# One granule's second FFN product as seven half-size products, in a fused attention and FFN kernel

## The chip, the cores and the metric

The kernel runs on one core of one Trainium2 chip. The metric is the device time in microseconds of one execution. All sets of timed runs here are of the fast state (the one not slowed by a lower TensorE clock), with a granted clock of 0.996 or more; the state of two single looks counts as unknown. The span in a profile is some 1.8 us shorter than the time of the same run. In the text PE is TensorE, PEld its loading of weights, DVE VectorE, ACT ScalarE, POOL GpSimd and SP the engine that issues most transfers, SPq its DMA queue.

## The reference

Attention with global and local keys, then an FFN with a squared relu, on 4 x 768 = 3072 tokens of width 512 and a hidden width of 2048:

```python
scores = q @ k.T / sqrt(64) + bias          # 8 heads; keys: 8 global ones, and the last 96
x = softmax(where(keep, scores, -1e9)) @ v  # heads side by side: 3072 x 512
h = x @ w_in                                # 512 -> 2048
g = s * maximum(h, 0)**2 + b
out = g @ w_out                             # 2048 -> 512
```

## The kernel before

Tokens are worked on in 12 granules of 256 (two blocks of 128). A granule passes through scores (L444), attention product (L504), normalisation on VectorE, a transposition of its result into `xT`, the first FFN product in eight chunks (L632), relu and square, and the second FFN product. From granule 4 on, pairs of granules do the second product in Strassen form (seven products where a plain one has eight, L832), for which sums of quarters of `w_out` (`weight_sums`) and of the data (`g_sum`) are made. Granules 0 to 3 do it plainly (L680). From granule 4 on the transposition is done by DMA:

```python
def x_by_dma(j):
    t = xT_tile(j)
    for i in range(GB):
        nc.sync.dma_start_transpose(t[:, :, i * P : (i + 1) * P], xn[j][:, i, :])

def p2_mm(j, tb, lo=0, hi=FC):              # plain second product of a block: L680
    ...
    for fc in range(lo, hi):
        nc.tensor.matmul(po[:], lhsT=g_of(j)[:, fc, tb * P : (tb + 1) * P],
                         rhs=w_out_bf[:, fc, :], start=(fc == 0), stop=(fc == FC - 1))

def finish_granule(j):
    ...                                     # x_by_pe for j < 4, else x_by_dma
    if 6 <= j + LEAD < NJ:
        hold_loads(xT[j][0:1, 0, GT - 1 : GT])   # GpSimd waits until xT has landed (L122)
        load_granule(j + LEAD)
```

`hold_loads` is of use to the reader: the start of GpSimd's small gate copy shows in the trace when granule j's transposes have landed. A `step(s, c0, c1, c2)` issues: scores of two units for step s+1, `c0`, an attention product, the output work put off until then (`flush`), `c1`, another attention product, `flush`, `c2`; at a granule's last step `finish_granule` comes after the first piece of `c2`. The steps in question:

```python
step(8, [lambda: rest(2, 0)] + late_p1(3, (0,)), late_p1(3, (1, 2)), late_p1(3, (3,)))
step(9, p2[2][1:2], late_p1(3, (4, 5)), late_p1(3, (6, 7)))            # finishes granule 4
step(10, p2[3][0:1], [lambda: shifted_template(range(H))], late[0:2] + [bias_diff], ps_h)
step(11, [lambda: p2_mm(3, 1, 0, FC // 2), u1(4, 0)], [u1(4, 1)],      # u1(4, 0): first use of xT 4
     late[2:4] + [shifted_copy, weight_sums[0]])
step(12, [lambda: rest(3, 1), u1(4, 2)], [weight_sums[1], u1(4, 3)], [weight_sums[2]])
```

The softmax here doesn't subtract the row's maximum and nothing guards it: scores larger than these inputs give would overflow.

## Time and profile before

| | before |
|---|---|
| time, median of 6 runs | 208.6 us (208.38 to 208.85) |
| span of the profile | 206.6 us |
| PE busy | 201.9 us |
| granule 4's first FFN matmul starts | 83.20 us |
| GpSimd's gate copy: granule 4's xT has landed | 82.96 us |

### The profile page before, as it was taken

The numbers are of one execution on the slowest core, as the hardware profiler recorded it, in microseconds if no ns is written. First come the engines' busy times: TensorE is split into PE (matmuls) and PEld (weight loads), VectorE is DVE, ScalarE is ACT, GpSimd is POOL, SyncE is SP. The second block draws the span as 40 slices with busy tenths as digits, with TensorE's granted clock in tenths as the row PEclk, the third lists the DMA queues.
The fourth block names the chain that finished last, engine by engine and source line by source line (L and its number), as shares of the span: only waits on it lengthen the run. The fifth ranks groups of instructions, "written<-read, shape, count | busy, mean of one in ns | idle before, by whom it ended". The sixth has DMA issues, their size and how long they took to land.

```text
span 206.6 us, 5313 instructions
## 1 busy us (share of the span) xinstructions
PE 201.9 (98%) x2182; PEld 160.1 (77%) x2190; DVE 160.9 (78%) x338; ACT 127.8 (62%) x197; POOL 69.9 (34%) x90
## 2 busy tenths in 40 slices
PE   8999999999999999999999999999999999999993
PEld 2678884557867585878888898888888889888883
DVE  7977589977989866799799975699866696737974
ACT  5766669486976558685664595663695764476200
POOL 8986333899454500913700907300000000000000
PEclk9999999999999999999999999999999999999999
DMA  5999999999999999999999999999570300240006
GB/s 163 173 179 201 207 206 178 156 153 130 130 147 119 156 121 218 208 195 214 148 205 149 116 125 212 167 219 77 53 206 3 98 9 0 61 145 0 0 10 197
DMA packets 110836, 28.17 MB, mean 136 GB/s; under 512 B 97852, under 2 KB 109308, under 8 KB 110812
## 3 DMA queue, kind: packets, MB, share of 16 engines
q0 software_dynamic: 76000, 13.11, 85.9%
q1 hardware_dynamic: 33612, 14.13, 41.0%
q10 hardware_dynamic: 1200, 0.59, 1.1%
q8 instruction: 17, 0.28, 0.6%
q14 instruction: 7, 0.06, 0.1%
HBM read 27.26 MB, written 6.29 MB: 162 GB/s over the span
## 4 chain that ended last, share of the span: by engine, by line
PE 95%; DMA 2%; DVE 1%; issue 0%; ACT 0%
PE ps L632 41%; PE ps L832 24%; PE ps L680 13%; PE ps_s L444 6%; PE ps_av L504 5%; DMA first<-in_k_dram 2%; PE ps_s L530 1%; PE ps_t L354 1%; PE ps_x L604 1%; PE ps_t L331 1%; PE ps_s L545 1%; PE ps_s L419 1%; PE ps_av L571 1%; PE ps_last L832 0%; PE ps_t L344 0%
## 5 line engine op out<-in xcount | busy, mean ns | idle before, releaser
L632 PE MATMUL ps<-xT,w_in_bf 128*128 128x256 bf16 x768 | 90.4, 273 | 0.1
L642 ACT ACTIVATE gT<-ps 128x512 bf16<-128x512 f32 x96 | 55.9, 598 | 47.9 <-PE ps L632 47.6
L632 PEld LDWEIGHTS <-w_in_bf 128*128 128x128 bf16 x768 | 73.1, 98 | 9.6 <-DVE xT L607 0.2
L453 ACT ACTIVATE pt<-ps_s 128x1024 bf16<-128x1024 f32 (+1 forms) x44 | 39.3, 946 | 3.2 <-PE ps_s L444 3.0
L680 PE MATMUL ps<-w_out_bf,gT 128*128 128x512 bf16 x120 | 28.7, 380 | 0.5 <-issue 0.2
L460 DVE TENSOR_TENSOR pt<-pt,tmpl 128x1024 bf16<-128x1024 bf16 (+1 forms) x40 | 24.4, 643 | 3.8 <-ACT pt L453 3.7
L832 PEld LDWEIGHTS <-gsum 128*128 128x128 bf16 x256 | 24.2, 98 | 3.7 <-DVE gsum L795 0.5
L108 POOL DMA_DIRECT2D vb<-in_v_dram x24 | 21.5, 910 | 5.5 <-DMA w_out_bf<-in_moe_w_out_dram 3.3
L806 DVE TENSOR_TENSOR gT<-gT 128x1024 bf16<-128x1024 bf16 x20 | 13.7, 686 | 11.7 <-ACT gT L642 11.7
L680 PEld LDWEIGHTS <-gT 128*128 128x128 bf16 x128 | 11.7, 98 | 13.0
L469 DVE TENSOR_TENSOR xn<-ps_av,rc 128x256 bf16<-128x256 f32 x48 | 20.4, 424 | 1.7
L832 PEld LDWEIGHTS <-gT 128*128 128x128 bf16 x200 | 18.6, 98 | 2.3
L468 DVE RECIPROCAL rc<-ps_av 128x4 f32<-128x4 f32 x48 | 8.5, 178 | 12.3 <-PE ps_av L504 10.8
L504 PEld LDWEIGHTS <-pt 128*128 128x128 bf16 x320 | 14.4, 97 | 2.7 <-DVE xn L469 0.7
L645 DVE TENSOR_TENSOR gT<-gT 128x512 bf16<-128x512 bf16 x32 | 13.0, 420 | 3.6 <-ACT gT L642 3.3
L504 PE MATMUL ps_av<-vb,pt 128*128 128x65 bf16 x208 | 15.3, 193 | 0.0
L832 PE MATMUL ps<-w_out_bf,gsum 128*128 128x256 bf16 x128 | 15.3, 273 | 0.0
L832 PE MATMUL ps<-wsub,gsum 128*128 128x256 bf16 x128 | 15.1, 273 | 0.0
L116 POOL DMA_DIRECT2D nat<-in_q_dram x14 | 12.4, 888 | 7.0 <-DMA vb<-in_v_dram 2.7
L122 POOL COPY gate<-xT 1x1 bf16<-1x1 bf16 x6 | 1.5, 250 | 37.1 <-DMA xT<-xn 37.1
L116 POOL DMA_DIRECT2D nat<-in_k_dram x14 | 12.4, 884 | 4.9 <-DMA w_in_bf<-in_moe_w_in_dram 2.4
L832 PE MATMUL ps<-w_out_bf,gT 128*128 128x256 bf16 x120 | 13.9, 273 | 0.0
(111 smaller groups left out, 230.5 us busy)
## 6 DMA issues: line engine op xcount, KB each, us to landing
out_dram<-o_q SPq DMA_DIRECT2D x15, 256.0 KB, 2.6
vb<-in_v_dram POOLq DMA_DIRECT2D x24, 128.0 KB, 8.8
nat<-in_k_dram POOLq DMA_DIRECT2D x22, 128.0 KB, 6.7
nat<-in_q_dram POOLq DMA_DIRECT2D x22, 128.0 KB, 6.9
w_out_bf<-in_moe_w_out_dram POOLq DMA_DIRECT2D x4, 512.0 KB, 16.2
w_in_bf<-in_moe_w_in_dram POOLq DMA_DIRECT2D x4, 256.0 KB, 7.5
w_in_bf<-in_moe_w_in_dram POOLq DMA_DIRECT2D x2, 512.0 KB, 11.2
out_dram<-o_sb SPq DMA_DIRECT2D x4, 256.0 KB, 6.1
```

The lines of the kernel that those rows point to most:

```text
L108: nc.gpsimd.dma_start(vbuf[b % 2][:, sb, :, 0:D], rows_of(v, b, sb))
L116: nc.gpsimd.dma_start(t[:, n, i, :, :], rows_of(srcs[n], b, sb))
L453: nc.scalar.activation(pt[:, :, 0:ncol], ps[:, :, 0:ncol], ACT.Exp, scale=QSCALE)
L460: nc.vector.tensor_tensor(pv, pv, m.rearrange("p h a c -> p h (a c)"), ALU.mult)
L469: nc.vector.tensor_tensor(dst, av[:, :, :, 0:D], rc[:].to_broadcast((P, 2, 2, D)), ALU.mult)
L504: nc.tensor.matmul(av[:, i, hi, 0 : D + 1], lhsT=pt[:, hi, c * P : (c + 1) * P], rhs=vv, start=(n == 0), stop=(n == len(terms) - 1),)
L632: nc.tensor.matmul(ps[:, i, :], lhsT=w_in_bf[:, kc, fc * P : (fc + 1) * P], rhs=xT[j][:, kc, :], start=(kc == 0), stop=(kc == KC - 1),)
L642: nc.scalar.activation(gs, ps[:], ACT.Relu)
L645: nc.vector.tensor_tensor(gs, gs, gs, ALU.mult)
L680: nc.tensor.matmul(po[:], lhsT=g_of(j)[:, fc, tb * P : (tb + 1) * P], rhs=w_out_bf[:, fc, :], start=(fc == 0), stop=(fc == FC - 1),)
L806: outs.append(lambda: nc.vector.tensor_tensor(gs, gs, gs, ALU.mult))
L832: nc.tensor.matmul(ps[:, tb, cs], lhsT=stat[:, fc, tb * P : (tb + 1) * P], rhs=mov[:, fc, cs], start=(fc == 0), stop=(fc == NH - 1),)
```

## The change

Granule 3's two blocks are taken as the two rows of a Strassen product by themselves: 7 products of 8 matmuls with 256 columns replace 2 x 16 matmuls with 512. The weight sums are therefore needed earlier, and so VectorE makes all four in stretches where it was idle. Two squares go to ScalarE, and four late outputs are put off to make room.

```diff
+    def sg_prod(n):
+        ...
+            for fc in range(NH):                       # 8 matmuls with 256 columns: L968
+                nc.tensor.matmul(ps, lhsT=stat[:, fc, :], rhs=mov[:, fc, :], ...)
+            outs.append(lambda: sg_evac(n, ps))
     ...
     finish_granule(2)
+    weight_sums[0]()
     ...
-    step(9, p2[2][1:2], late_p1(3, (4, 5)), late_p1(3, (6, 7)))
-    step(10, p2[3][0:1], [lambda: shifted_template(range(H))], late[0:2] + [bias_diff], ps_h)
+    step(9, [weight_sums[1]] + p2[2][1:2], [sg_sum(3)] + act_p1(3, (4, 5)),
+         late_p1(3, (6,)) + [weight_sums[2]] + late_p1(3, (7,)) + [flush, sg_sum(1)])
+    step(10, [sg_prod(7), sg_prod(1), sg_prod(2)],
+         [bias_diff, lambda: shifted_template(range(H)), sg_prod(5)], [sg_sum(4)], pre=[sg_sum(2)])
     step(
         11,
-        [lambda: p2_mm(3, 1, 0, FC // 2), u1(4, 0)],
-        [u1(4, 1)],
-        late[2:4] + [shifted_copy, weight_sums[0]],
+        [sg_prod(6), u1(4, 0)],
+        [sg_join(1), weight_sums[3], u1(4, 1)],
+        [sg_join(0), sg_join(2), shifted_copy] + late[0:2],
     )
-    step(12, [lambda: rest(3, 1), u1(4, 2)], [weight_sums[1], u1(4, 3)], [weight_sums[2]])
+    step(12, [sg_prod(3), sg_prod(4), u1(4, 2)], [u1(4, 3)], late[2:4])
```

More of the change, by code (lines that the diff above doesn't have):

```diff
@@ L921, in join, with sg_half, sg_sum, go @@
         return go
+    SG = 3
+    sg = {}
+    def sg_half(half, tb):
+        return g_of(SG)[:, half * NH : (half + 1) * NH, tb * P : (tb + 1) * P]
+    def sg_sum(n):
+        def go():
+            if not sg:
+                for i, key in ((2, (3, 1)), (3, (2, 4))):
+                    t = gpool.tile([P, 2, NH, P], BF16, name="sgsum", tag=f"gsum{i}", bufs=1)
+                    for a, m in enumerate(key):
+                        sg[m] = t[:, a]
+            dst, x, y, op = {
+                1: (sg[1], sg_half(0, 1), sg_half(1, 1), ALU.add),
+                2: (sg[2], sg[1], sg_half(0, 0), ALU.subtract),
+                3: (sg[3], sg_half(0, 0), sg_half(0, 1), ALU.subtract),
+                4: (sg[4], sg_half(1, 0), sg[2], ALU.subtract),
+            }[n]
+            nc.vector.tensor_tensor(dst, x, y, op)
+        return go
@@ new lines, with go @@
+    sg_ps = {}
+    sg_r = {}
+    def sg_prod(n):
+        def go():
+            stat = {
+                1: lambda: sg_half(0, 0),
+                2: lambda: sg_half(1, 0),
+                3: lambda: sg[4],
+                4: lambda: sg_half(1, 1),
+                5: lambda: sg[1],
+                6: lambda: sg[2],
+                7: lambda: sg[3],
+            }[n]()
+            mov = {1: w11, 2: w21, 3: w22, 4: t4, 5: t1, 6: t2, 7: t3}[n]
+            bank, c = {1: (0, 0), 7: (0, 1), 2: (1, 0), 5: (2, 0), 6: (4, 0), 3: (3, 0), 4: (3, 1)}[n]
+            if bank not in sg_ps:
+                sg_ps[bank] = ps_h.tile([P, GB, CH], F32, name="ps_2", tag="psh")
+            ps = sg_ps[bank][:, c, :]
+            for fc in range(NH):
+                nc.tensor.matmul(
+                    ps, lhsT=stat[:, fc, :], rhs=mov[:, fc, :], start=(fc == 0), stop=(fc == NH - 1)
+                )
+            outs.append(lambda: sg_evac(n, ps))
+        return go
@@ new lines, in sg_store, with sg_evac @@
+    def sg_store(tb):
+        b, g = divmod(SG, NGR)
+        t0 = b * S + g * GT + tb * P
+        nc.sync.dma_start(out[t0 : t0 + P, :], sg_r["out", tb][:])
+    def sg_evac(n, ps):
+        if not sg_r:
+            p0, p1_, p2_ = (
+                work.tile([P, GB, CH], F32, name=f"part{i}", tag=f"part{i}", bufs=1)
+                for i in range(3)
+            )
+            sg_r.update({0: p0[:, 0, :], 6: p0[:, 1, :], 1: p1_[:, 0, :], 7: p2_[:, 0, :]})
+            for tb in range(GB):
+                sg_r["out", tb] = work.tile([P, DM], F32, name="o_sb", tag="o_sb", bufs=3)
+        if n == 1:
+            scaled(sg_r[0], ps, bvec[:, 0:CH])
+        elif n == 2:
+            scaled(sg_r["out", 0][:, 0:CH], ps, sg_r[0])
+        elif n == 5:
+            scaled(sg_r[1], ps, bdiff[:])
+        elif n == 6:
+            scaled(sg_r[6], ps, sg_r[0])
+        elif n == 7:
+            nc.scalar.activation(sg_r[7], ps, ACT.Copy, scale=s_bc[:])
+        elif n == 3:
+            scaled(sg_r["out", 0][:, CH:DM], ps, sg_r[1])
+            sg_store(0)
+        elif n == 4:
+            scaled(sg_r["out", 1][:, 0:CH], ps, sg_r[6])
+            sg_store(1)
@@ L923, in pe, with sg_join, go @@
+    def sg_join(n):
+        def go():
+            if n == 1:
+                add_f32(sg_r[1], sg_r[1], sg_r[6])
+            elif n == 0:
+                add_f32(sg_r[6], sg_r[6], sg_r[7])
+            else:
+                add_f32(sg_r["out", 1][:, CH:DM], sg_r[7], sg_r[1])
+        return go
     def pe(pr, n):
@@ L942, in go, with act_p1 @@
             outs.append(square)
+        return [lambda fp=fp: go(fp) for fp in fps]
+    def act_p1(j, fps):
+        def go(fp):
+            relu, _ = p1_mm(j, fp)
+            relu()
+            gs = g_of(j)[:, 2 * fp : 2 * fp + 2, :]
+            nc.scalar.activation(gs, gs, ACT.Square)
         return [lambda fp=fp: go(fp) for fp in fps]
@@ L1167 @@
     step(8, [lambda: rest(2, 0)] + late_p1(3, (0,)), late_p1(3, (1, 2)), late_p1(3, (3,)))
-    step(9, p2[2][1:2], late_p1(3, (4, 5)), late_p1(3, (6, 7)))
-    step(10, p2[3][0:1], [lambda: shifted_template(range(H))], late[0:2] + [bias_diff], ps_h)
+    step(
+        9,
+        [weight_sums[1]] + p2[2][1:2],
+        [sg_sum(3)] + act_p1(3, (4, 5)),
+        late_p1(3, (6,)) + [weight_sums[2]] + late_p1(3, (7,)) + [flush, sg_sum(1)],
+    )
+    step(
+        10,
+        [sg_prod(7), sg_prod(1), sg_prod(2)],
+        [bias_diff, lambda: shifted_template(range(H)), sg_prod(5)],
+        [sg_sum(4)],
+        pre=[sg_sum(2)],
+    )
     step(
         11,
-        [lambda: p2_mm(3, 1, 0, FC // 2), u1(4, 0)],
-        [u1(4, 1)],
-        late[2:4] + [shifted_copy, weight_sums[0]],
+        [sg_prod(6), u1(4, 0)],
+        [sg_join(1), weight_sums[3], u1(4, 1)],
+        [sg_join(0), sg_join(2), shifted_copy] + late[0:2],
     )
-    step(12, [lambda: rest(3, 1), u1(4, 2)], [weight_sums[1], u1(4, 3)], [weight_sums[2]])
+    step(12, [sg_prod(3), sg_prod(4), u1(4, 2)], [u1(4, 3)], late[2:4])
     for pr in range(2, NJ // 2):
@@ L1192 @@
             [u1(o, 3), g_sum(pr, 1, 0)],
-            [g_sum(pr, 1, 1), pe(pr, 7), g_sum(pr, 2)] + [weight_sums[3]] * (pr == 2),
+            [g_sum(pr, 1, 1), pe(pr, 7), g_sum(pr, 2)],
             pre=[g_sum(pr, 3, 1)],
```

## The prediction

> **What bounds the kernel now.** I read the page's engine table first, then the chain that ended last, then the same chain in order of time around the second FFN product of granule 3, and last the timelines of VectorE, the transposing DMA queue and GpSimd for the same microseconds.
>
> ```profile
> PE 201.9 (98%) x2182; PEld 160.1 (77%) x2190; DVE 160.9 (78%) x338; ACT 127.8 (62%) x197; POOL 69.9 (34%) x90
> PE 95%; DMA 2%; DVE 1%; issue 0%; ACT 0%
> ```
>
> TensorE (PE) is busy 98% and is 95% of the chain. After the first 5 us nothing holds it up: the list of waits has no PE matmul wait above 0.2 us. So a microsecond of PE work taken away is a microsecond gained, unless PE then arrives too early for something else. The chain in order of time shows the work that the change touches (start, length, what):
>
> ```profile
> 76.49 0.55 PE ps_s L444 x16
> 77.04 0.32 PE ps L680
> 77.36 0.05 issue
> 77.42 3.19 PE ps L680 x14
> 80.60 0.48 PE ps_av L504 x16
> 81.09 0.44 PE ps_s L444 x12
> 81.53 1.62 PE ps L680 x7
> 83.15 0.05 issue
> 83.20 1.91 PE ps L632 x16
> 85.11 0.24 PE ps_av L504 x8
> 85.35 1.75 PE ps L632 x16
> ...
> 87.78 0.16 issue
> 87.94 1.67 PE ps L680 x7
> ```
>
> The L680 pieces are granule 3's product: block 0 from 77.04 to 80.60, the first half of block 1 from 81.53 to 83.20, its second half from 87.78 to 89.61. At 83.20 the first FFN matmul of granule 4 (L632) starts, on an xT that the DMA queue transposes. Two lines say when that xT is there:
>
> ```profile
> 75.45 2.52 SPq L612 DMA_TRANSPOSE xT<-xn  x2
> 82.96 0.47 POOL L122 COPY gate<-xT 1x1 bf16<-1x1 bf16 x1 [12.65 <-DMA xT<-xn]
> ```
>
> The two transposes are issued from 75.45 on, and GpSimd, which sat 12.65 us waiting for the second of them, gets on at 82.96. PE wants it at 83.20, so it is there only 0.24 us before it is needed. That margin is hidden in the profile of before (PE shows no wait), and I take it for the number that decides this case.
>
> **What the Trainium skill says.** "TensorE: Matmul & The Clock Gate", section "Back-to-back issue gap", lists 262 cycles for 256 columns and 518 for 512 at 2.4 GHz, so 109 and 216 ns: halving the columns costs almost nothing. The trace agrees: 16 matmuls of 256 columns take 1.75 us, 109 ns each; block 0's 16 of 512 take 3.56 us, 222 ns. (The same section's sustained figure of 131 ns for 512 columns is not what this trace shows.) "VectorE: DVE Perf Modes", section "The perf-mode tier table", has a bf16 tensor_tensor of 2048 elements at 1224 ns; the weight sums of this trace took 1215 to 1218 ns. "DMA: Bandwidth & Descriptors", section "Issuing engines are not separate DMA queues", says transfers from all issuing engines run on the same 16 DMA engines; the DMA row is at 9 in nearly every slice until two thirds of the span, and the transposes of granule 4 took about 6 us from issue to landing in that crowd.
>
> **The change, part by part.**
>
> *PE, the gain.* Gone are 2 x 16 matmuls of 512 columns: 3.56 + 1.67 + 1.83 = 7.06 us on the chain. Added are 7 products of 8 matmuls of 256 columns: 56 x 109 ns = 6.12 us. The weights loaded rise from 32 to 56, at 98 ns each, under the 109 ns of the matmul beside them. PE work falls by 0.94 us by the chain; by pure pitch it is 8 x 109 = 0.87 us. I use 0.87.
>
> *Where it is gained.* In place of block 0 (3.56 us) PE now does products 7, 1, 2 and 5, 32 x 109 ns = 3.50 us: next to nothing. In place of block 1's first half (1.67 to 1.75 us) it does product 6 alone, 0.87 us: here is the gain. In place of the second half it does products 3 and 4, 1.75 for 1.83 us. So nearly all of the gain falls due just before granule 4's first matmul, which PE would now reach at about 82.35.
>
> *The new wait.* Nothing in the change makes granule 4's transposes earlier. They need the last attention output of granule 4, which VectorE writes from 75.00 (reciprocal at 74.78, both set by PE); what stands before them in that DMA queue is the same. So the xT lands at about 82.9 again, and PE can start at about 83.0 to 83.1 rather than 82.35: some 0.7 us of the 0.87 are lost. Left: 83.20 - 83.05 = 0.15 us, and about 0.07 us from the second half, together 0.2 us.
>
> *VectorE, added.* Between 71.7 and 80 us it gets two weight sums (1.14 us each from start to start, as in the trace), three 1024-element sums (0.60 to 0.68 each) and loses two squares that go to ScalarE (0.75). Idle there was:
>
> ```profile
> 72.79 0.18 DVE L468 RECIPROCAL rc<-ps_av 128x4 f32<-128x4 f32 x1 [1.05 <-PE ps_av L504]
> 74.78 0.18 DVE L468 RECIPROCAL rc<-ps_av 128x4 f32<-128x4 f32 x1 [0.69 <-PE ps_av L504]
> 76.28 0.43 DVE L645 TENSOR_TENSOR gT<-gT 128x512 bf16<-128x512 bf16 x1 [0.19 <-ACT gT L642]
> 77.16 0.42 DVE L645 TENSOR_TENSOR gT<-gT 128x512 bf16<-128x512 bf16 x1 [0.45 <-ACT gT L642]
> 80.88 0.18 DVE L468 RECIPROCAL rc<-ps_av 128x4 f32<-128x4 f32 x1 [1.20 <-PE ps_av L504]
> ```
>
> Following its new order by hand: masks end at 71.67; first sum to 72.81, where the reciprocal was due at 72.79; normalisation and output to 74.03; sum 3 to 74.63, due 74.78; normalisation to 75.34; sum of w12 in place to 76.48; the two last squares, held by their relu, to 77.58; sums 1 and 2 to 79.0; masks to 80.2; normalisation to 80.8. Against PE: product 7 needs the w12 sum at 77.04 (0.5 us to spare), product 2 the squares at 78.8 (1.2), product 5 sum 1 at 79.9 (1.6), and the next attention product needs that normalisation at 80.8 (nothing to spare: a wait of up to 0.1 us, which the xT wait swallows). The evacuations that product 6 and granule 4 wait for come at about 81.1 and 81.4, with 0.4 us or more to spare. The first weight sum, now after granule 2's transposition, takes 1.14 us of a VectorE pause of 1.04 us that ends at 51.26; PE uses that result only from 53.1. The fourth goes from 110 to about 86 us and is due at product 4, near 88.4 (0.8 to spare). To make room, the four late outputs (0.66 us each) are moved back.
>
> *ScalarE.* Two squares, about 0.6 us each, before the relu of the last two chunks; it had pauses of 0.28, 0.52 and 0.28 us, then 77.02 is reached as before. No effect on PE.
>
> *DMA.* The four stores of late outputs now all go behind granule 5's transposes in the queue, where three went ahead. Those transposes landed by 96.24 for a need at 97.64, and now come earlier.
>
> **The rivals.** *(A) The full gain:* the transposes land early enough, because the crowd on the DMA engines happens to clear sooner. Then 208.57 - 0.87 = 207.7. For it: the time to landing is a matter of what else is in flight, and 0.5 us is small beside 6. Against: all traffic ahead of it is unchanged. *(B) VectorE becomes the bound* in the stretch from 76 to 81 us: each step there lies within 0.1 to 0.5 us of its need, and a slip of 0.5 us at product 7 or the attention product adds that much, then 208.6 to 209.0. For it: 78% busy before, and 95% in this stretch after. Against: the hand-made order has PE need each result later than it comes, and the first 0.6 us of such a slip only takes the place of the xT wait. *(C) A slip of the attention output of granule 4* (VectorE held up by the first two sums at 72 to 75 us) moves the transposes and with them granule 4: as much loss as slip, up to 0.3 us, so 208.6 at most.
>
> **Range and chances.** The expected sum is 208.57 - 0.2 = 208.35. Weights by judgement: the xT wait as worked out 0.65, (A) or part of it 0.15, (B) or (C) 0.2. That gives 207.7 to 208.75 for 8 in 10. A gain of 2% would be 4.2 us, over four times the PE work removed: ruled out. A loss of 2% needs a wait of 4 us or more, which nothing in the profile offers.
>
> **What would show it.** In the profile after: PE busy falls by about 0.9 us while the span falls by much less; the 120 recorded matmuls of 512 columns at L680 become some 90, and 56 of 256 appear; PE's list of waits gains one of 0.5 to 0.7 us at L632, put down to the DMA of xT, and GpSimd's gate copy stands again near 83.0 with L632 right behind it. Wrong would be: L632 of granule 4 at 82.4 with no wait (A); a PE wait on VectorE at the new products or at the attention product after them (B); the SP transposes issued later than 75.5 (C).

## More of the kernel before

How full VectorE is in the stretch that the change fills shows in the view of stretches (the columns are the length, then the busy time of PE, PEld, DVE, ACT and POOL; the last three are the granted clock, the DMA engines' share and GB/s):

```profile
70.00:81.00 11.00, 10.95 (x107) 7.12 (x106) 6.63 (x15) 6.67 (x15) 0.31 (x1) 1.00 1.78 171
```

PE is busy for 10.95 of the 11 us, VectorE (third pair) for 6.63.

## The result, and the profile after

The median is 208.5 us (six runs, 207.65 to 209.18) against 208.6 (208.38 to 208.85). The ratio is 0.9994, with a 95% interval of 0.997 to 1.0017. A ratio is the mean time of one kernel's fast runs over that of the other's of the same rounds, so not quite the ratio of the medians. It is the same time within the noise, inside the predicted range. One thing stands out that the prediction had not named: the changed kernel's runs spread over 1.5 us, those of before over 0.5.

The page of the changed kernel:

```profile
PE 201.0 (97%) x2209; PEld 162.0 (78%) x2214; DVE 165.2 (80%) x347; ACT 129.3 (63%) x200; POOL 69.9 (34%) x90
...
PE 92%; DMA 5%; DVE 1%; issue 0%; SPq 0%
...
L632 PE MATMUL ps<-xT,w_in_bf 128*128 128x256 bf16 x768 | 90.4, 273 | 0.7 <-DMA xT<-xn 0.7
```

PE is busy 0.9 us less, and the span is no shorter (206.8 us). The DMA's share of the chain rose from 2% to 5%, and the first FFN product has an idle time of 0.7 us ahead of it, ended by the DMA of xT, where it had 0.1:

```profile
L632 PE MATMUL ps<-xT,w_in_bf 128*128 128x256 bf16 x768 | 90.4, 273 | 0.1
```

PE's timeline shows where (start, length, what; in brackets the idle time before and what ended it), and GpSimd's and the queue's say why:

```profile
77.05 1.05 PE L968 MATMUL ps<-w_out_bf,sgsum 128*128 128x256 bf16 x8
77.94 1.91 PE L968 MATMUL ps<-w_out_bf,gT 128*128 128x256 bf16 x16
...
79.93 1.03 PE L968 MATMUL ps<-wsub,sgsum 128*128 128x256 bf16 x8
...
81.71 1.05 PE L968 MATMUL ps<-wsub,sgsum 128*128 128x256 bf16 x8
83.42 1.91 PE L632 MATMUL ps<-xT,w_in_bf 128*128 128x256 bf16 x16 [0.66 <-DMA xT<-xn]
```
```profile
75.53 2.52 SPq L612 DMA_TRANSPOSE xT<-xn  x2
```
```profile
83.34 0.35 POOL L122 COPY gate<-xT 1x1 bf16<-1x1 bf16 x1 [12.91 <-DMA xT<-xn]
```

The transposes are issued at 75.53, as before (75.45). They have landed when GpSimd gets on at 83.34, and PE starts 0.08 us later. The wait of 0.66 us is counted from the end of the matmul before it, at 82.76, and the records of matmuls overlap. In the profiles below without a wait, L632 starts 0.87 to 0.89 us after product 6, which here would be 82.6: PE lost some 0.8 us. Granule 4 starts 0.22 us later than in the kernel before (PE was 0.08 us late at product 7), so the wait took the whole gain and a little more. The chain in order of time leaves PE there and goes through the transposes and what let them be issued:

```profile
75.08 0.42 DVE xn L469
75.50 1.14 DVE w_out_bf L768
76.64 0.10 SPq L612
76.75 0.05 issue
76.80 6.49 DMA xT<-xn
83.29 0.14 issue
83.42 1.91 PE ps L632 x16
```

The DVE line L768, a weight sum, is in this chain by its time alone: the transposes don't read its result. They need the normalisation that ended at 75.50, after which the first was issued. The 6.49 us are those of the second.

VectorE's stretch filled up as intended:

```profile
70.00:81.00 11.00, 11.00 (x119) 8.41 (x118) 10.62 (x20) 8.13 (x19) 0.43 (x1) 1.00 1.76 169
```

It went from 6.63 to 10.62 of 11 us. The weight load of the attention product after product 5 did wait for it:

```profile
80.92 0.29 PEld L504 LDWEIGHTS <-pt 128*128 128x128 bf16 x8 [0.24 <-DVE xn L469]
```

### The profile page after: what moved, and what is told of

Read it like the earlier page. It is cut to its first block, busy times and chain, and to the rows that moved or that the text cites. A ratio compares the mean times of both kernels' runs of the same rounds, so it can differ in the third digit from the quotient of the medians.

```text
span 206.8 us, 5376 instructions
## 1 busy us (share of the span) xinstructions
PE 201.0 (97%) x2209; PEld 162.0 (78%) x2214; DVE 165.2 (80%) x347; ACT 129.3 (63%) x200; POOL 69.9 (34%) x90
## 4 chain that ended last, share of the span: by engine, by line
PE 92%; DMA 5%; DVE 1%; issue 0%; SPq 0%
PE ps L632 40%; PE ps L832 24%; PE ps L680 10%; PE ps_s L444 5%; PE ps_av L504 5%; DMA xT<-xn 3%; DMA first<-in_k_dram 2%; PE ps_s L530 1%; PE ps L968 1%; PE ps_t L354 1%; PE ps_s L419 1%; PE ps_x L604 1%; PE ps_t L331 1%; PE ps_s L545 1%; DVE w_out_bf L768 1%; PE ps_av L571 1%
## 5 line engine op out<-in xcount | busy, mean ns | idle before, releaser
L632 PE MATMUL ps<-xT,w_in_bf 128*128 128x256 bf16 x768 | 90.4, 273 | 0.7 <-DMA xT<-xn 0.7
L632 PEld LDWEIGHTS <-w_in_bf 128*128 128x128 bf16 x768 | 72.9, 98 | 10.0 <-DMA xT<-xn 0.9
L680 PE MATMUL ps<-w_out_bf,gT 128*128 128x512 bf16 x91 | 21.8, 379 | 0.3
L832 PEld LDWEIGHTS <-gT 128*128 128x128 bf16 x200 | 18.6, 98 | 2.3
L680 PEld LDWEIGHTS <-gT 128*128 128x128 bf16 x96 | 8.9, 98 | 9.6
L645 DVE TENSOR_TENSOR gT<-gT 128x512 bf16<-128x512 bf16 x30 | 12.2, 421 | 3.1 <-ACT gT L642 2.7
```

The costliest lines, as they stand in the source:

```text
L632: nc.tensor.matmul(ps[:, i, :], lhsT=w_in_bf[:, kc, fc * P : (fc + 1) * P], rhs=xT[j][:, kc, :], start=(kc == 0), stop=(kc == KC - 1),)
L645: nc.vector.tensor_tensor(gs, gs, gs, ALU.mult)
L832: nc.tensor.matmul(ps[:, tb, cs], lhsT=stat[:, fc, tb * P : (tb + 1) * P], rhs=mov[:, fc, cs], start=(fc == 0), stop=(fc == NH - 1),)
```

## The experiments

My theory: the saved PE work is real, but granule 4's first FFN matmul now waits for transposes that land no earlier. Rivals: VectorE's fuller stretch took the gain back; or the seven products save less PE time than counted. Times are medians of six runs unless noted, beside the kernel before on the same chip. Its median was 208.43 beside the first four kernels, 208.49 beside the next four and 208.73 to 208.75 beside the last.

### Take away what granule 4 waits for

In the changed kernel and in the kernel before, granule 4's first two chunks read granule 3's xT. Their outputs are wrong, which doesn't matter for the times.

```diff
-                    rhs=xT[j][:, kc, :],
+                    rhs=xT[3 if j == 4 and fp < 2 else j][:, kc, :],
```

> The changed kernel, with granule 4's first two FFN chunks reading granule 3's xT, which has long landed (wrong result on purpose). Theory (the gain is lost waiting for granule 4's transposes): the 0.66 us PE wait at L632 put down to the DMA of xT is gone, PE has no new wait over 0.2 us, and the time falls by 0.6 to 0.9 us against the changed kernel and against the kernel before, to about 207.8. Rival (VectorE's longer work, or PE's own pitch, took the gain back): the time stays within 0.2 us of the changed kernel's 208.5.

> The kernel before with the same replacement (wrong result on purpose), as a control. Theory: the transposes land 0.2 us before they are needed there, so the median is within 0.15 us of before. A rival that has every kernel here held up by xT has it fall as much as the changed kernel does.

The changed kernel came to 207.97 us (207.63 to 209.04), ratio to before 0.998 (0.996 to 1.000): faster by some 0.4 us, at the edge of the noise. This is less than expected, but in the theory's direction. PE had no wait at L632, and granule 4 started at 82.78. That profile alone proves little: its own transposes had landed by 81.99, so there would have been no wait without the edit either. The kernel before with the same edit came to 208.73 (ratio 1.0007, interval across 1); the median is 0.3 above its control of 208.43, more than the 0.15 expected, and so is no gain at all. Its transposes landed at 83.72, after PE's start at 83.46, so this run of the kernel before would have waited too. The profiled run of the changed kernel was its slowest, 209.04, and shows another transfer arriving late, 26 us on:

```profile
108.83 0.57 PE L444 MATMUL ps_s<-qx,kx 64*128 64x128 bf16 x14 [1.05 <-DMA qx<-nat]
```

This is the query transpose of granule 8, which was in time in the profiles before and after. So one wait removed does not make all later landings safe, and not all of the scatter of the runs comes from granule 4.

### Let the transposes overtake two stores

The edit keeps the result right: granule 2's two 256 KB output stores, so far ahead of granule 4's transposes in SP's queue, are issued behind them.

```diff
+        put_out = lambda: nc.sync.dma_start(out[t0 : t0 + P, :], o_sb[:])
+        if j == 2:
+            behind.append(put_out)
+        else:
+            put_out()
     ...
             finish_granule(j)
+            while behind:
+                behind.pop(0)()
```

> The changed kernel with granule 2's two 256 KB output stores issued after granule 4's transposes instead of ahead of them (right result). In the profile each store ahead took about 0.9 us of the queue's landings. Theory: granule 4's xT lands 1 us or more earlier than 83.3, before PE wants it at about 82.7; the wait is gone and the time falls by 0.6 to 0.9 us, to about 207.8, and the runs spread less than the 1.5 us of the changed kernel. Rival (landing is set by the loads of the GpSimd queue beside it, not by the stores ahead): xT lands within 0.3 us of 83.3 and the time stays.

> The kernel before with the same two stores behind the transposes (right result). Theory: the median stays within 0.15 us of before, as nothing there waits for xT in the usual run.

The changed kernel with it: 207.67 us, ratio 0.9961 (0.9948 to 0.9974), and its six runs lie within 0.4 us. The kernel before with it: 208.39, ratio 0.9996 (0.9984 to 1.0007). Only the changed kernel gains, 0.72 us between the two. GpSimd's line and PE's line of the changed kernel with the edit:

```profile
81.63 0.18 POOL L122 COPY gate<-xT 1x1 bf16<-1x1 bf16 x1 [10.99 <-DMA xT<-xn]
```
```profile
77.20 1.05 PE L973 MATMUL ps<-w_out_bf,sgsum 128*128 128x256 bf16 x8
78.09 1.91 PE L973 MATMUL ps<-w_out_bf,gT 128*128 128x256 bf16 x16
80.08 1.03 PE L973 MATMUL ps<-wsub,sgsum 128*128 128x256 bf16 x8
81.42 0.51 PE L444 MATMUL ps_s<-qx,kx 64*128 64x128 bf16 x12
81.86 1.05 PE L973 MATMUL ps<-wsub,sgsum 128*128 128x256 bf16 x8
82.75 0.49 PE L632 MATMUL ps<-xT,w_in_bf 128*128 128x256 bf16 x3
```

and the same stretch of the kernel before with the edit:

```profile
77.11 3.63 PE L680 MATMUL ps<-w_out_bf,gT 128*128 128x512 bf16 x16
...
81.60 1.90 PE L680 MATMUL ps<-w_out_bf,gT 128*128 128x512 bf16 x8
83.34 0.93 PE L632 MATMUL ps<-xT,w_in_bf 128*128 128x256 bf16 x7
```

A landing at 81.63, and at 81.34 in the kernel before with the edit, is no proof by itself: without the edit landings from 81.41 on are seen too (below). The three profiles with the edit have 81.63, 81.34 and 79.90, a mean of 81.0 against 82.4 in eight without it, and all six timed runs of the changed kernel take less than 208 us.

The landing comes first in both now, so this pair shows the size of the PE saving alone. From the first product to granule 4: 83.34 - 77.11 = 6.23 us against 82.75 - 77.20 = 5.55 us, so 0.68 us saved. This version beats the kernel before by 0.4%, clear of the noise. Its interval just meets that of the changed kernel (0.997 to 1.0017), taken in other rounds. The spread is the clearer sign: eleven runs with the stores behind (these six and the five with the moved sum below) lie between 207.58 and 208.18 us, twelve of the changed kernel between 207.65 and 209.83.

### Make the suspected cost larger

One more 256 KB copy, on the chip and read by nobody, ahead of the transposes in the same queue, in both kernels.

```diff
         if last:
+            if j == 4:
+                extra = const.tile([P, 2 * DM], BF16, name="extra")
+                nc.sync.dma_start(extra[:], w_in_bf[:, 0, 0 : 2 * DM])
             finish_granule(j)
```

> The changed kernel with one more 256 KB copy (on-chip, into a tile nobody reads; right result) ahead of granule 4's transposes in the same queue: the suspected cost raised. Theory: xT lands 0.6 to 1.2 us later than 83.3, PE waits that much longer at L632 (1.2 to 1.9 us in all) and the time rises by 0.5 to 1.2 us to about 209.3. Rival (what limits the changed kernel lies elsewhere): the time stays within 0.2 us of 208.5.

> The kernel before with the same extra copy. Theory: its margin of 0.2 us is used up first, so PE now shows a wait at L632 of 0.4 to 1.0 us and the time ends beside that of the changed kernel with the extra copy, within 0.3 us of it: both then start granule 4 at the same landing.

The changed kernel: 209.16 us, but from 208.06 to 209.84, ratio to before 1.0013 (0.9987 to 1.004), so the rise is not clear of the noise. The kernel before: 209.80 (209.16 to 210.16), ratio 1.0054 (1.0038 to 1.0069), which is clear. In the profiles granule 4 starts at 84.27 and 84.53, each 0.08 or 0.09 us behind its gate copy, and both kernels now wait: PE 1.50 us in the changed one, 0.86 us in the other. The first of these is put down by the profile to a mask of VectorE; PE's weight load names the DMA of xT. So in these profiles a later landing delays both kernels, and the kernel before has less far to go. That the two medians would meet within 0.3 us was missed: they differ by 0.64. Two of the changed kernel's runs took 208.1, as if the copy had cost nothing. There is no trace of these, so why the copy delayed the kernel before more regularly stays open.

### Take other traffic away

Granule 7's two V loads, which GpSimd's queue had in flight beside the transposes, are issued after granule 4's xT has landed.

```diff
-        load_v(j)                    # in load_granule
+        if j != 7:
+            load_v(j)
     ...
             hold_loads(xT[j][0:1, 0, GT - 1 : GT])
+            if j == 4:
+                load_v(7)
```

> The changed kernel with granule 7's two V loads (GpSimd's queue, landing at 80.9 and 83.1 beside the transposes) issued only after granule 4's xT has landed (right result). If these loads share the landing time with the transposes: xT lands 0.5 us or more before 83.3, the wait shrinks or goes, and the time falls by 0.4 to 0.9 us. If only what stands ahead in the same queue counts: xT lands within 0.2 us of 83.3 and the time stays near 208.5.

207.91 us, ratio 0.9976 (0.9955 to 0.9996), an interval that still holds the changed kernel's 0.9994. xT landed at 80.17 by the gate copy, over 1 us below the earliest of the eight profiles without such an edit. It is one profile, but it speaks for the other queue's traffic counting as well. Three runs took 207.60, three 208.2 to 208.8. The profiled one of these shows the wait in a new place, at granule 6 (the edit moves L632 to L633):

```profile
114.25 1.92 PE L633 MATMUL ps<-xT,w_in_bf 128*128 128x256 bf16 x16 [0.49 <-DMA xT<-xn]
```

The delayed loads are one difference between this kernel and those in which granule 6 did not wait. That they delayed its transposes is likely, not shown.

### The sums alone

The kernel before, with the first two weight sums and the two squares placed as in the change, and the plain product.

```diff
     finish_granule(2)
+    weight_sums[0]()
     ...
-    step(9, p2[2][1:2], late_p1(3, (4, 5)), late_p1(3, (6, 7)))
+    step(9, [weight_sums[1]] + p2[2][1:2], act_p1(3, (4, 5)), late_p1(3, (6, 7)))
     ...                                     # both sums are gone from steps 11 and 12
```

> The kernel before with two of the change's four moves of weight sums (the first after granule 2's transposition, the second in the step before the last chunks) and its two squares on ScalarE, but the plain product. Rival B (VectorE's added work in that stretch costs PE time): slower by 0.2 us or more. Theory: within 0.15 us of before, no PE wait on VectorE.

208.34 us (five runs, within 0.2), ratio 0.9989, and no PE wait on VectorE after the first transpositions. These moves cost nothing. The other part of VectorE's load, the in-place sum and the data sums, can't be had without the seven products, so it was tried from the other side:

### Relieve VectorE where PE waited for it

On top of the stores put behind, the second data sum moves from ahead of the masks to behind the next normalisation.

```diff
-        [sg_prod(7), sg_prod(1), sg_prod(2)],
+        [lambda: outs.append(sg_sum(2)), sg_prod(7), sg_prod(1), sg_prod(2)],
     ...
-        pre=[sg_sum(2)],
```

> The changed kernel with the two stores behind the transposes, and besides with its second data sum moved from ahead of the masks to behind the next attention normalisation on VectorE (right result). In the profile of the version without this move the next attention product's weight load waits 0.24 us for that normalisation. If this wait is the part of the PE saving that is still missing (0.68 of 0.87 us arrived), the weight load's wait goes, granule 4 starts 0.1 to 0.15 us earlier and the time is 207.5 to 207.6. If the missing part lies elsewhere, or the sum now delays product 6, the time is within 0.1 us of 207.67.

207.98 us (five runs), ratio 0.9966: no gain over the 0.9961 without it. The weight load's wait of 0.24 us is gone, but the wait went one product further. Product 6 needs a PSUM buffer that VectorE evacuates after the moved sum:

```profile
81.34 0.48 DVE L846 SCALAR_TENSOR_TENSOR part<-ps,s_bc,bvec 128x256 f32<-128x256 f32 x1
```
```profile
81.23 0.51 PE L444 MATMUL ps_s<-qx,kx 64*128 64x128 bf16 x12
81.88 1.03 PE L973 MATMUL ps<-wsub,sgsum 128*128 128x256 bf16 x8
```

The evacuation ends at 81.82 and the product starts at 81.88, 0.65 us after the scores; it was 0.44 us after them without the move. Granule 4 starts at 82.75 in both.

### The changed kernel again

Unaltered, for its scatter: two looks, and six more runs.

> The changed kernel once more, unaltered, for a second pair of landing and time. In five profiles with this queue order so far the second transpose of granule 4 landed between 81.4 and 83.7 us. Theory: granule 4 starts at the later of 82.75 and the landing plus 0.14 us, and the profiled span is 206.1 us plus the excess over 82.75, within 0.2 us; if the span does not follow the landing in this way, something else moves it too.

> The same kernel a third time, with the same expectation: the start of granule 4 at the later of 82.75 and the landing plus 0.14 us, and the span 206.1 us plus the excess over 82.75, within 0.2 us.

> The changed kernel unaltered, timed again: how often does its wait for granule 4's transposes occur? In the six runs of the first measurement the time went from 207.65 to 209.18 us; two later looks, both with an early landing and no wait, took 207.93 and 207.99. Theory: the single runs fall between 207.6 and 209.2 with the landing, so they spread over 0.8 us or more while before spreads less, and the median lies between 207.8 and 208.6, not lower than the 207.67 of the version with the stores behind.

| profile of the changed kernel | gate copy | PE wait | granule 4 starts | span |
|---|---|---|---|---|
| first | 83.34 | 0.66 | 83.42 | 206.8 |
| second | 81.90 | none | 82.78 | 206.2 |
| third | 82.28 | none | 82.84 | 206.2 |
| fourth | 81.94 | none | 83.01 | 206.4 |

The second's landing and start:

```profile
81.90 0.44 POOL L122 COPY gate<-xT 1x1 bf16<-1x1 bf16 x1 [11.32 <-DMA xT<-xn]
82.78 1.91 PE L632 MATMUL ps<-xT,w_in_bf 128*128 128x256 bf16 x16
```

The rule was made from the first profile and others with early landings. The second and third follow it, but both landed early, so of its two halves they test one: an early landing, no wait and no loss. One profile in four shows the wait. In the fourth, granule 4 started 0.26 us later than the rule says. PE was late there well before (first FFN matmul at 14.68 instead of the first profile's 14.28, product 7 at 77.46 where the other three have 77.05 to 77.30), so that is not the landing's doing. The two looks took 207.93 and 207.99 us, and the six runs had a median of 208.25, from 207.71 to 209.83, ratio 0.9992 (0.9961 to 1.0023). One run lies above the 209.2 that I expected as the upper end; it has no trace.

## Why the prediction was right, and which sizes were off

**The bound and the place of the wait: right.** PE's busy time fell by 0.9 us and the span did not. The wait came where it was expected, at granule 4's first FFN matmul, put down to xT, at 0.66 us for a predicted 0.5 to 0.7. That the profiled run showed it was in part luck: three later profiles of the same kernel have no such wait. Taking the wait's cause away, by order in the queue, gave about the time that rival A had named: 207.67 for 207.7.

**The PE gain: 0.87 us predicted, 0.68 us measured.** In the pair with the stores behind, the work itself behaves as counted: up to granule 4, 24 matmuls with 512 columns took 3.47 + 1.74 = 5.21 us, and 40 with 256 took 2.63 + 0.90 + 0.89 = 4.42 us, so 0.79 us less. (The 3.56 us for the first 16, 222 ns each, in the prediction come from pieces of the chain and are 0.09 too high.) The prediction put 0.80 of its 0.87 here and 0.07 in the second half. By its own count all 0.87 belongs here, as the second half has the same number of columns before and after (8 matmuls of 512, 16 of 256). Of the measured 0.79, 0.09 us go to the wait for the normalisation: for product 5 I took the 0.90 us of the run in which nothing waits behind it, and with the wait it is 0.99 us from product 5 to the attention product. The prediction had named that wait "up to 0.1 us", and let the xT wait swallow it; where the landing is early it counts in full. And the second half's 0.07 us did not come: products 3 and 4 took 1.76 us, the plain half 1.74 in the pair. The 1.83 us in the prediction was read from a piece of the chain with 0.16 us of "issue" ahead of 7 recorded matmuls where there are 8, so most likely the eighth is missing from the trace.

**The landing: taken as fixed, which it is not.** The step "xT lands at about 82.9 again" is the one that was mis-sized. In eight profiles with this queue order and this traffic (the two kernels, both with xT replaced, the sums alone, and three more of the changed kernel) the gate copy started between 81.41 and 83.72, a range of 2.3 us. Counted from the issue of the first transpose (75.36 to 75.94), five landings come after 6.0 to 6.5 us and three after 7.5 to 8.0, with none between. PE needs xT 7.75 us after that issue in the kernel before and 7.06 in the changed one (83.20 - 75.45 and, in the second profile above, 82.78 - 75.72). So the change moved the need from within the late group to between the two: an early landing costs nothing, a late one brings the wait. Why a landing is early or late is not shown. In the three late profiles the second of granule 7's V loads, on GpSimd's queue, also landed late (82.5 to 83.8 us, against 80.1 to 81.3 in the five), so both queues are late together. The wait thus comes in some runs and not in others, which is likely the main part of the changed kernel's spread of 1.5 us (2.1 the second time). Of its twelve timed runs two have a trace, and only one of these (208.56 us) shows the wait, so for the others this is not shown. The fastest run, 207.65, has about the full gain. That the changed kernel's median is close to that of before is in part chance: 208.5 the first time, 208.25 the second.

**VectorE (rival B): refuted as the main cause.** The order worked out by hand held: the sum of w12 done at 76.63 for a predicted 76.5, the two squares at 77.66 for 77.58, the normalisation at 80.86 for 80.8. With the same VectorE work and an early landing the kernel takes 207.67. **Rival C: did not occur.** The transposes were issued at 75.53; PE itself was 0.08 us later than before by then.

## What to carry to other kernels

When the bounding engine has no waits, look up for each of its inputs how long before the need it arrives: work saved just ahead of such an input is worth no more than that margin. If the input is a transfer, its landing can scatter (by 2.3 us in eight profiles here), so take several profiles; and try first to let it overtake what stands ahead of it in its queue, which here cost nothing and turned a gain of nothing into 0.4%.

## What the Trainium skill lacked or had wrong

- "DMA: Bandwidth & Descriptors", section "Latency and other measured facts", gives effective bandwidths for DMA transposes and no scatter of their landing beside other traffic. Here the same pair of transposes, issued at the same place, had landed between 81.41 and 83.72 us in eight profiles; with two 256 KB stores put behind them, three profiles have 79.90 to 81.63.
- "TensorE: Matmul & The Clock Gate", section "Back-to-back issue gap": its sustained figure of 131 ns for 512 columns is not seen; 16 of them took 3.47 us, 217 ns each, which is its figure for a single gap. With 256 columns 24 took 2.63 us, 110 ns each.
- "VectorE: DVE Perf Modes", section "The TRN2 errata": its formula for a PSUM source, 120 cycles and one per element at 0.96 GHz, makes 392 ns for 256 elements and 658 for 512, by my estimate. The records of the evacuations with a second operand last longer, 470 to 480 and about 745 ns, but the next record of VectorE starts before they end: 0.40 us after the start at 82.57 (256 elements, changed kernel) and 0.66 us after that at 81.44 (512, kernel before). So the formula fits the spacing of instructions here and not their recorded length; the section doesn't say which of the two its PSUM column gives.
